# Drains of GpSimd behind every second row scatter of chunks 1 to 3, in place of register loads, in a fused Sinkhorn attention and mixture-of-experts kernel

## Chip, cores and metric

One core of a Trainium2 chip. The metric is the device time of one execution in microseconds (us), as the median of a kernel's runs. Two kernels are compared by the ratio of the mean time of one kernel's fast runs to that of the other's fast runs of the same rounds, so a ratio is not quite the ratio of the medians quoted beside it. "Faster", "same" and "slower" are set at 2%. Engine names in the profiles: PE is TensorE (PEld its weight loads), DVE VectorE, ACT ScalarE, POOL GpSimd, SP SyncE; POOLq is GpSimd's sequencer.

## What is computed

```python
# attention, B=4 H=8 S=768 D=64, 8 blocks of 96 rows
for _ in range(5):                       # Sinkhorn normalisation of sort_net -> P
    P = exp(P - max); P /= sum over rows; P /= sum over columns
k_sorted, v_sorted = P @ blocks of k, P @ blocks of v
attn_out = softmax(q_block @ k_sorted_block.T / sqrt(D)) @ v_sorted_block
x = attn_out as (3072, 512)
# mixture of experts, E=8, F=1024, one expert a row
e_idx = argmax(x @ w_gate + modality_bias[modality_id]); gate = softmax at e_idx
out[rows of e] = gate * (relu(x[rows of e] @ w1[e]) @ w2[e])
```

## The kernel before

The 3072 rows are made in four chunks of 768 (m = 0 to 3). Attention writes a chunk's rows into a row buffer `xb`, of which there are two; `place(m)` works out the row number in a scratch tensor for each row and scatters the chunk there with eight indirect DMAs from GpSimd. Rows of one expert then lie together. Slots (up to 256 rows of one expert) are read back with transposing DMAs on SP and go through the expert's two matrix products, which are laid between the later units of attention. Cuts are marked `# ...`.

```python
xb = [singles.tile([BLK, 8, GW], BF16, ...) for z in range(2)]      # two row buffers
small = ctx.enter_context(tc.tile_pool(name="small", bufs=1))       # one buffer unless said

def av(u):                                   # unit u of attention, 8 units a chunk
    xt = xb[(u // 8) % 2]
    # ... PE: op = attnT x v_sb
    nc.vector.reciprocal(rs, ...)                                    # L443
    nc.vector.tensor_tensor(xt[...], ov[...], rs..., ALU.mult)       # L444: writes the row buffer

def place(m):
    xt = xb[m % 2]
    dest = small.tile([BLK, 8], I32, tag="dest", ...)                # list of rows, one buffer
    # ... DVE works out dest; GpSimd puts the row's number into xt
    def one(t):
        if t:
            if m:
                for _ in range(2):
                    nc.gpsimd.reg_load(pause, etab[0:1, 0:1])        # L536
            nc.gpsimd.nop()
        ins = nc.gpsimd.indirect_dma_start(                          # L538
            out=xs_dram, out_offset=IndirectOffsetOnAxis(ap=dest[:, t:t + 1], axis=0),
            in_=xt.bitcast(I32)[:, t], in_offset=None)
        after = []                                                   # extra waits: none
        # ... the scatters are declared independent of each other
    for t in range(8):
        one(t)

def x_fetch(s, ...):                         # slot s, on SP, behind the chunk's scatters
    nc.sync.dma_start_transpose(out=xT_b[s % NX][...], in_=...)      # L661

def late_w1():                               # 2 MB of weights of the second expert, from GpSimd
    # ... load_w(1), behind the load of slot 1
at1(9, place, 0); at1(18, place, 1); at1(26, place, 2)               # at which unit of attention
at2(12, late_w1)                             # so the weights are issued just ahead of chunk 1's rows
```

The softmax here doesn't subtract the row's maximum and nothing guards it: scores larger than these inputs give would overflow.

Of the kernel before, what the change touches and what calls it, by code (L numbers as in the profile page):

```python
# [17 lines left out]
def kernel(  # L18
# [13 lines left out]
    nc = tc.nc  # L32
# [153 lines left out]
    etab = singles.tile([1, E], I32)  # L186
# [152 lines left out]
    def use(act=0.0, dve=0.0):  # L339
        busy[0] += act  # L340
        busy[1] += dve
# [150 lines left out]
        oh_t[m] = (oh, ls)  # L492

    scat = {}
    pause = nc.gpsimd.alloc_register("pause")
    ones_ = {}
    mark = [None]

    def place(m):
        oh, ls = oh_t[m]  # L500
        xt = xb[m % 2]
        prev = ohs[m % 2]
        rk = mipsum.tile([128, 8, E], FP32, tag="mi", name=f"rk{m}")
        rkf = rk.rearrange("p t e -> p (t e)")
        pb = bass.AP(tensor=prev.tensor, offset=prev.offset, ap=[prev.ap[0], [0, 8], prev.ap[1]])
        nc.tensor.matmul(rkf, maskUT[0:BLK, :], oh.rearrange("p t e -> p (t e)"), start=True, stop=False,
                         skip_group_check=True)
        nc.tensor.matmul(rkf, ones_bf[0:BLK, :], ebase.rearrange("p t e -> p (t e)"), start=False, stop=False,
                         skip_group_check=True)
        nc.tensor.matmul(rk, ones_bf[0:BLK, :], pb, start=False, stop=False, skip_group_check=True)  # L510
        for t in range(7):
            ob = bass.AP(tensor=oh.tensor, offset=oh[:, t].offset, ap=[oh.ap[0], [0, 7 - t], [1, E]])
            nc.tensor.matmul(rk[:, t + 1:8], ones_bf[0:BLK, :], ob, start=False, stop=(t == 6),
                             skip_group_check=True)
        sel_r = small.tile([BLK, 8, E], FP32, tag="selr", name=f"selr{m}")
        nc.vector.tensor_tensor(sel_r, rk[0:BLK], oh, ALU.mult)
        dest = small.tile([BLK, 8], I32, tag="dest", name=f"dest{m}")
        dstf = small.tile([BLK, 8], FP32, tag="dstf", name=f"dstf{m}")
        nc.vector.tensor_reduce(dstf, sel_r, AX.X, ALU.add)
        nc.vector.tensor_copy(dest, dstf)  # L520
        sm = small.tile([BLK, 8, 1], FP32, tag="sm", name=f"sm{m}")
        nc.vector.tensor_reduce(sm, ls, AX.X, ALU.add)
        gcol = xt.bitcast(FP32)[:, :, Dm // 2 + 1:Dm // 2 + 2]
        nc.vector.reciprocal(gcol, sm)
        g, hf = m // 2, m % 2
        icol = xt.bitcast(I32)[:, :, Dm // 2]
        idm = idI.rearrange("p (b f j) -> p b f j", b=4, f=2)[:, 2 * g:2 * g + 2, hf]
        nc.gpsimd.tensor_copy(icol.rearrange("p (r j) -> p r j", r=2), idm)
        scat[m] = []
        use(dve=1.5)  # L530

        def one(t):
            if t:
                if m:
                    for _ in range(2):
                        nc.gpsimd.reg_load(pause, etab[0:1, 0:1])  # L536
                nc.gpsimd.nop()
            ins = nc.gpsimd.indirect_dma_start(  # L538
                out=xs_dram, out_offset=bass.IndirectOffsetOnAxis(ap=dest[:, t:t + 1], axis=0),
                in_=xt.bitcast(I32)[:, t], in_offset=None)  # L540
            after = []
            tc.declare_no_dep(ins.ins, group="xs", reason="rows are disjoint", **({"keep": after} if after else {}))
            tc.add_to_no_dep_group("xs", ins.ins)
            for pre in after:
                tc.add_manual_dep(ins.ins, pre.name, SYNC, reason="rows leave at an even pace")
            scat[m].append(ins.ins)
        ones_[m] = one
        for t in range(8):
            one(t)
        nxt = ohs[(m + 1) % 2]  # L550
        ohsum = small.tile([BLK, E], FP32, tag="ohsum", name=f"ohsum{m}")
        nc.vector.tensor_reduce(ohsum, oh.rearrange("p t e -> p e t"), AX.X, ALU.add)
        nc.vector.tensor_tensor(nxt, ohsum, prev, ALU.add)
# [484 lines left out]
```

## Time and profile before

| | before |
|---|---|
| runs before the prediction | 193.73 us median (192.12 to 194.36, 3 runs) |
| profiled execution | 230.75 us, span 229.1 us, mean granted clock 0.856 |
| PE busy in the profile | 174.5 us |

The profiled execution is 37 us longer than the timed ones. Its run is not among them. In the timelines below a line is: start, duration, engine, source line, operation and tiles, count, and in brackets how long the engine had been idle and what ended that.

### The profile page before, as it was taken

To read this page: it belongs to the slowest core of one execution; us is meant where nothing else is said; L and a number is where in the kernel's file an instruction comes from. 1 tells how busy PE (TensorE), PEld (TensorE's weight loads), DVE (VectorE), ACT (ScalarE), POOL (GpSimd) and SP (SyncE) were. 2 spreads that over 40 slices of the span, in tenths; PEclk is the share of its full clock that TensorE was granted. 3 is DMA by queue.
4 is the path that set the end of the run, shared out by engine and by line. 5 is a ranking of instruction groups with operands and counts; after the bars stand their busy time and mean duration, and the time that the engine had idled before them with its cause. 6 is when DMAs were issued, how large, how long until landed. Compare 5 with 4: busy or idle time off the path is not lost.

```text
span 229.1 us, 5357 instructions
## 1 busy us (share of the span) xinstructions
PE 174.5 (76%) x2127; PEld 127.6 (56%) x2127; DVE 100.7 (44%) x332; ACT 93.4 (41%) x149; POOL 83.3 (36%) x118
## 2 busy tenths in 40 slices
PE   6573978876399986399954599933969999999930
PEld 6473877664299964167641477620456676675410
DVE  5877479643077885127740355430122322322200
ACT  2135678573178871356631544302223232232320
POOL 7801869406510317430177003572301322322330
PEclk9889799995557999569985599985799999999996
DMA  5999999999907399270032622452324346122210
GB/s 62 196 226 198 212 223 222 188 226 204 249 28 72 45 193 231 66 178 9 0 112 75 138 50 92 98 171 107 98 72 107 83 121 118 57 81 94 94 46 0
DMA packets 30164, 27.71 MB, mean 121 GB/s; under 512 B 18831, under 2 KB 25775, under 8 KB 29872
## 3 DMA queue, kind: packets, MB, share of 16 engines
q0 software_dynamic: 11792, 23.10, 45.2%
q1 hardware_dynamic: 18336, 4.16, 10.7%
q8 instruction: 19, 0.31, 0.5%
q14 instruction: 17, 0.14, 0.2%
HBM read 27.35 MB, written 10.52 MB: 165 GB/s over the span
## 4 chain that ended last, share of the span: by engine, by line
PE 33%; issue 27%; DMA 16%; DVE 9%; POOL 8%; another core or an unknown queue 1%; ACT 1%; POOLq 1%; DVEq 0%; ACTq 0%
DMA kvb<-in_v_dram 8%; DMA xs_scratch<-xb,dest 8%; POOL out_dram L708 6%; PE hp L694 6%; PE yp L717 5%; PE va L374 5%; DVE xb L444 4%; PE sc L417 4%; PE gt L453 4%; PE op L436 3%; PE lg L463 2%; PE tq L236 1%; PE ka L365 1%; POOL xs_scratch L538 1%
## 5 line engine op out<-in xcount | busy, mean ns | idle before, releaser
L708 POOL DMA_INDIRECT out_dram<-kvb,idg x25 | 24.5, 981 | 80.0 <-ACT kvb L704 38.2
L694 PE MATMUL hp<-xT,w 128*128 128x256 bf16 x384 | 49.1, 278 | 4.6 <-issue 2.5
L694 PEld LDWEIGHTS <-w 128*128 128x128 bf16 x384 | 36.7, 99 | 14.0 <-issue 6.1
L538 POOL DMA_INDIRECT xs_scratch<-xb,dest x32 | 29.4, 919 | 29.6 <-issue 27.4
L717 PE MATMUL yp<-w,hT 128*128 128x512 bf16 x96 | 26.9, 428 | 7.6 <-ACT hT L688 7.6
L423 ACT ACTIVATE attnT<-sc 96x768 bf16<-96x768 f32 x32 | 25.9, 810 | 15.0 <-PE sc L417 6.0
L717 PE MATMUL yp<-w,qT 128*128 128x512 bf16 x96 | 22.5, 379 | 0.0
L444 DVE TENSOR_TENSOR xb<-op,rs 96x512 bf16<-96x512 f32 x32 | 22.0, 687 | 1.2
L417 PE MATMUL sc<-qT,kT 64*128 64x96 bf16 (+1 forms) x256 | 13.8, 222 | 9.6 <-issue 6.1
L717 PEld LDWEIGHTS <-hT 128*128 128x128 bf16 x96 | 9.7, 106 | 20.0 <-ACT hT L688 9.3
L688 ACT ACTIVATE hT<-hp 128x512 bf16<-128x512 f32 x17 | 10.0, 595 | 26.4 <-remote 14.6
L706 DVE TENSOR_SCALAR kvb<-yp,idg 128x512 f32<-128x512 f32 x10 | 7.5, 751 | 29.5 <-PE yp L717 26.6
L704 ACT ACTIVATE kvb<-yp,idg 128x512 f32<-128x512 f32 x14 | 9.6, 687 | 22.8 <-PE yp L717 19.4
L688 ACT ACTIVATE qT<-hp 128x512 bf16<-128x512 f32 x16 | 9.5, 595 | 18.2 <-PE hp L694 18.1
L436 PE MATMUL op<-v_sb,attnT 96*128 96x65 bf16 x256 | 14.6, 204 | 2.6 <-DVE xb L444 2.0
L374 PE MATMUL va<-bd,kvb 128*128 128x128 bf16 x128 | 14.1, 283 | 2.3 <-DMA kvb<-in_v_dram 2.3
L352 ACT CAST kT<-ka 128x512 bf16<-128x512 f32 (+1 forms) x17 | 10.1, 639 | 14.0 <-PE ka L365 8.0
L417 PEld LDWEIGHTS <-kT 64*128 64x128 bf16 (+1 forms) x256 | 8.0, 102 | 13.6 <-issue 11.6
L717 PEld LDWEIGHTS <-qT 128*128 128x128 bf16 x96 | 9.2, 98 | 9.3
L374 PEld LDWEIGHTS <-kvb 128*128 128x128 bf16 x128 | 12.9, 189 | 2.6 <-DMA kvb<-in_v_dram 2.4
L453 PE MATMUL gt<-ident,xb 96*128 96x96 bf16 x128 | 9.6, 224 | 5.7 <-DVE xb L444 4.6
L436 PEld LDWEIGHTS <-attnT 96*128 96x128 bf16 x256 | 11.5, 105 | 3.3 <-DVE xb L444 2.5
(182 smaller groups left out, 233.3 us busy)
## 6 DMA issues: line engine op xcount, KB each, us to landing
w<-in_moe_w_dram POOLq DMA_DIRECT2D x4, 1024.0 KB
kvb<-in_k_dram POOLq DMA_DIRECT2D x4, 768.0 KB
kvb<-in_v_dram POOLq DMA_DIRECT2D x2, 1536.0 KB
q_in<-in_q_dram POOLq DMA_DIRECT2D x4, 384.0 KB
xs_scratch<-zpad SPq DMA_DIRECT2D x3, 258.0 KB
v_sb<-in_q_dram POOLq DMA_DIRECT2D x4, 192.0 KB
v_sb<-in_q_dram POOLq DMA_DIRECT2D x2, 384.0 KB
xs_scratch<-xb,dest POOLq DMA_INDIRECT x32
```

Of the source, the lines that this page charges most:

```text
L352: (nc.scalar.copy if pick(act, dve) else nc.vector.tensor_copy)(dst, src)
L374: nc.tensor.matmul(acc[:, z], v_cols[:, d0 + z], bd[g], start=True, stop=True)
L417: nc.tensor.matmul(sc[0:m, par, j * BLK:(j + 1) * BLK], kT[g][rows, x0:x0 + m], qT[rows, i], start=True, stop=True)
L423: mark[0] = nc.scalar.activation(attnT[u % 2][:, 0:8 * BLK].rearrange("p (r f) -> p r f", r=2), sc_tiles.pop(u)[0:BLK, :, 0:4 * BLK], ACT. ...
L436: nc.tensor.matmul(ov[:, par, j], attnT[u % 2][:, c0:c0 + 128], v_sb[g][0:BLK, par * 64 + h * 8 + i, 0:D + 1], start=True, stop=True)
L444: nc.vector.tensor_tensor(xt[:, :, h * D:(h + 1) * D].rearrange("p (r j) d -> p r j d", r=2), ov[0:BLK, :, :, 0:D], rs.broadcast_to([BLK, ...
L453: nc.tensor.transpose(tp[:, t], xb[m % 2][:, t, c * 128:(c + 1) * 128], ident[:BLK, :BLK])
L538: ins = nc.gpsimd.indirect_dma_start(out=xs_dram, out_offset=bass.IndirectOffsetOnAxis(ap=dest[:, t:t + 1], axis=0), in_=xt.bitcast(I32)[: ...
L688: mark[0] = nc.scalar.activation(dst, src, ACT.Relu)
L694: nc.tensor.matmul(hp[:, f], w_at(s, c * F + (2 * j + f) * 128, 128), xT_b[s % NX][:, c], start=(c == 0), stop=(c == 3))
L708: ins = nc.gpsimd.indirect_dma_start(out=out, out_offset=bass.IndirectOffsetOnAxis(ap=idg[:, t, 0:1], axis=0), in_=y, in_offset=None, boun ...
L717: nc.tensor.matmul(yp, hT_b[s % 2][:, fc, t * 128:(t + 1) * 128], w_at(s, 4 * F + fc * Dm, Dm), start=(fc == 0), stop=(fc == 7))
```

## The change

The register loads were meant to space a chunk's scatters. They are replaced by a `drain` of GpSimd before scatters 2, 4 and 6 of chunks 1, 2 and 3, nine in all, which should hold each further pair back until the engine is idle.

```diff
-    pause = nc.gpsimd.alloc_register("pause")
...
         def one(t):
             if t:
-                if m:
-                    for _ in range(2):
-                        nc.gpsimd.reg_load(pause, etab[0:1, 0:1])
+                if m and t % 2 == 0:
+                    nc.gpsimd.drain()
                 nc.gpsimd.nop()
```

Later lines move up by two: the drain is L534, the scatter L536, the slot load L659, the first expert product L692 (L694 before).

## The prediction

> **What bounds the kernel now.** I read the page first (shares by engine, slices), then the groups and the timeline of Pool for the scatters, then the uses and loads of the slots' tiles, then the timeline of PE and the busy times by window.
>
> Page, shares, slices and two groups:
>
> ```profile
> span 229.1 us, 5357 instructions
> PE 174.5 (76%) x2127; PEld 127.6 (56%) x2127; DVE 100.7 (44%) x332; ACT 93.4 (41%) x149; POOL 83.3 (36%) x118
> PE   6573978876399986399954599933969999999930
> POOL 7801869406510317430177003572301322322330
> ...
> L538 POOL DMA_INDIRECT xs_scratch<-xb,dest x32 | 29.4, 919 | 29.6 <-issue 27.4 <-DMA w<-in_moe_w_dram 2.0 <-POOL xb L528 0.3
> ```
>
> PE is the busiest engine. Its row of slices has four holes, and each lies under a run of sevens and fives of Pool: the row scatters of chunks 0 to 3. From slice 30 on PE is at nine tenths: the expert tail is bound by PE.
>
> Pool's timeline, four scatters of chunk 1 and the end of it:
>
> ```profile
> 84.86 0.98 POOL L538 DMA_INDIRECT xs_scratch<-xb,dest  x1 [5.58 <-issue]
> 86.14 0.95 POOL L538 DMA_INDIRECT xs_scratch<-xb,dest  x1 [0.30 <-issue]
> 87.39 0.91 POOL L538 DMA_INDIRECT xs_scratch<-xb,dest  x1 [0.30 <-issue]
> 88.61 0.91 POOL L538 DMA_INDIRECT xs_scratch<-xb,dest  x1 [0.30 <-issue]
> ...
> 93.46 0.90 POOL L538 DMA_INDIRECT xs_scratch<-xb,dest  x1 [0.30 <-issue]
> 97.18 1.01 POOL L708 DMA_INDIRECT out_dram<-kvb,idg  x1 [2.82 <-ACT kvb L704]
> ```
>
> A scatter takes 0.91 us on Pool and the next starts 0.30 us later, 1.21 us from start to start; eight take 93.46 + 0.90 - 84.86 = 9.50 us. Chunk 0, which has no register loads between its scatters, is no faster: in the same timeline its later ones start at 56.47, 57.70 and 58.92, 1.22 us apart. So the loads already cost nothing that Pool shows. The line of the loads says why:
>
> ```profile
> L536 POOLq EVENT_SEMAPHORE  x42: 17/17/17, 84.6 to 148.4; - x42
> L645 POOLq TENSOR_LOAD <-etab x3: 298/300/514, 34.8 to 62.8; - x3
> ```
>
> 42 = 3 chunks x 7 gaps x 2, so each register load is there only as a semaphore increment of 17 ns; a real load (of the weights' expert number, second line) is a TENSOR_LOAD of 300 ns. I read this as loads into a register that nobody reads, of which the compiler left only the count. The last increment is at 148.4 while the last scatter starts at 153.1: Pool's sequencer runs several scatters ahead of the engine, so whatever it does between them is hidden.
>
> **What the Trainium skill says.** (1) "Perfetto Trace Analysis", section "DMA Instruction — SWDGE (GPSIMD)": the sequencer is free once it has pushed such a DMA to the wait queue, and its recorded end is where the last descriptor is written, not where data lands. The trace agrees: the 4.7 us of run-ahead above, and records of 0.91 us against a median of 3.4 us to landing for the transfers of this scratch tensor. (2) "PSUM — Partial Sum Buffer", section "Engine vs sequencer instructions": a nop is the sequencer's alone and waits only for dispatch; "drain waits for the engine to go fully idle". No drain lies between the scatters of this trace, so its cost isn't shown here. (3) "DMA: Bandwidth & Descriptors", section "Latency and other measured facts": a floor of about 600 ns for a tensor_load. The trace has 300 ns for a real one and 17 ns for what is left of the pauses; the measurement decides, and removing them saves nothing.
>
> **The change, part by part.** Removed: 42 register loads, 42 x 17 ns = 0.7 us of a sequencer that is ahead anyway. On the path: 0.
>
> Added: drains before scatters 2, 4 and 6 of three chunks, nine in all. A drain stops the run-ahead: the next scatter is decoded only once the engine is idle. What a scatter costs from cold is in the trace at the head of each chunk: the vector engine writes the row numbers (timeline of DVE, line L520) from 83.50 for 0.17 us, and the first scatter of chunk 1 starts at 84.86, 1.19 us later; in chunk 3 143.28 + 0.17 to 144.62, 1.17 us. Part of that is the hand-over between engines, which a drain hasn't got. Against 0.30 us for a queued one a drain therefore costs at most 1.19 - 0.30 = 0.9 us; I choose two thirds, 0.6 us, as an estimate. Per chunk 3 x 0.6 = 1.8 us: eight scatters take 9.5 + 1.8 = 11.3 us. Over three chunks Pool is 5.4 us longer at work.
>
> Does it reach the end? Two things wait for a chunk's scatters: the loads of its slots on SP, and the output scatters behind them on Pool. Timeline of SP, the first load after chunks 1, 2 and 3, and below it the landing time from the view of this tile:
>
> ```profile
> 96.02 1.27 SPq L661 DMA_TRANSPOSE xT<-xs_scratch  x1
> 126.18 1.14 SPq L661 DMA_TRANSPOSE xT<-xs_scratch  x1
> 158.94 1.27 SPq L661 DMA_TRANSPOSE xT<-xs_scratch  x1
> DMA to landing us min/median/max: 3.2/4.3/5.5
> ```
>
> Landed about 100.3, 130.5 and 163.2. A slot takes 32 matmuls of line L694, so counting them in PE's timeline tells when a slot is first used: slot 2 (chunk 1), slot 4 (chunk 2), slot 8 (chunk 3):
>
> ```profile
> 115.92 1.05 PE L694 MATMUL hp<-xT,w 128*128 128x256 bf16 x8
> 146.80 3.65 PE L694 MATMUL hp<-xT,w 128*128 128x256 bf16 x32
> 183.63 1.91 PE L694 MATMUL hp<-xT,w 128*128 128x256 bf16 x16
> ```
>
> Slack: 15.6, 16.3 and 20.4 us. Against 1.8 us of delay (2.7 at most) nothing is late. The output scatters: one stands right behind chunk 2 (at 124.59) and two behind chunk 3 (154.34, 155.64), each with only 0.30 us of wait, so they slip by 1.8 us too; they read one of eight result buffers, and a buffer is written again four slots later, over 25 us on. Slack again. On the path: 0. The view of the chain that ended last does put 18.2 us on the transfer of chunk 3's rows, up to 170.38; I don't follow it there, since the Pool instruction at its end (174.44, L708) waits for a DVE result by Pool's own timeline. It is an inferred releaser.
>
> **The holes of PE.** Are they a cost in the timed runs, which the drains could change? In the profile PE advances in single matmuls 0.7 us apart during chunk 2, with "issue" as its wait, and ACT and DVE stand still too, until the scatters are over. By windows, the four holes:
>
> ```profile
> 50.00:64.00 14.00, 7.85 (x140) 6.13 (x141) 4.07 (x13) 5.08 (x9) 7.47 (x8) 0.52 1.12 213
> 84.00:97.00 13.00, 6.88 (x77) 4.22 (x76) 4.93 (x22) 3.79 (x7) 7.37 (x8) 0.79 0.76 155
> 115.00:129.00 14.00, 5.88 (x69) 3.69 (x69) 3.00 (x14) 3.83 (x6) 8.16 (x9) 0.64 0.40 112
> 150.00:160.00 10.00, 2.41 (x11) 0.62 (x9) 1.28 (x11) 1.68 (x3) 5.10 (x6) 0.65 0.45 146
> ```
>
> Columns: window, length, then busy time of PE, PEld, DVE, ACT, POOL, granted clock, DMA share, GB/s. PE idles 6.2 + 6.1 + 8.1 + 7.6 = 28.0 us there, and 229.1 - 174.5 - 28.0 = 26.6 us elsewhere. The timed runs have a median of 193.73 us, 35.4 us less than the profile. With PE's 174.5 us of work that leaves 19.2 us idle, less than the 26.6 us outside the holes. So in the timed runs the holes are largely or wholly gone: they come, I infer, with the taking of the profile. Then slack shrinks by the part of a hole that lies between scatter and use, at most 8 us, and stays above 7 us.
>
> **Rivals.** (a) The holes are in part real, and a burst of scatters starves the other engines. Then a break behind every second scatter lets them in. For: the code's own remark that rows should leave at an even pace, and holes exactly under the bursts, also where the DMA share is only 0.40. Against: the sum above. If 8 us of holes in chunks 1 to 3 were real and half went, the time would be 189.7 us. (b) The drain also waits for the rows to land, or restarts expensively. Then it costs about 3.4 us instead of 0.6, 3 x 3.4 = 10.2 us a chunk, which eats the reduced slack of chunk 1 (15.6 - 6 = 9.6 us) and perhaps of chunk 2, and the time would be 194.5 to 199 us. Against: a Pool instruction's record ends with its descriptors, and idle means the engine, not the transfers. (c) The stretched bursts leave the 2 MB load of the second expert's weights, which is in flight beside chunk 1, freer: its share of the DMA is mixed with the scatters between 84 and 94. It is used first at 102, so early arrival buys nothing: 193.7 us.
>
> **Range and chances.** Main path 0 us; I take 0.2 us off for rival (a) weighed against (b): 193.5 us. The three timed runs of before span 192.12 to 194.36, 1.2%, so noise alone takes a median about 1.5 us to either side; rival (a) stretches the range below to 190.3, rival (b) above to 196.5. Faster by over 2% (below 189.9) needs most of rival (a): 0.11. Slower by over 2% (above 197.6) needs rival (b) in full: 0.08. Within 2%: 0.81.
>
> **What would show it.** Right: the line of the loads is gone; scatters 2, 4 and 6 of chunks 1 to 3 start about 0.9 us after the end of the one before instead of 0.30, the others stay at 0.30; a chunk's eight take 11 to 12 us; slots 2, 4 and 8 still land over 5 us before their first matmul; PE has no new wait for the slots' tile; the tail from slot 5 on is as long as before. Wrong: gaps of 3 us or more at the drains (rival b), or timed runs below 190 us with PE's holes in chunks 1 to 3 shorter (rival a). A profile whose span moves while the timed runs don't would confirm that the holes belong to the profile.

## The result and the profile after

| | before | after |
|---|---|---|
| median of 4 runs | 193.22 us (192.12 to 194.36) | 199.74 us (198.78 to 202.02) |
| ratio | | 1.0321, 95% interval [1.0231, 1.041]: slower |
| profiled execution | span 229.1 us, clock 0.856 | span 200.3 us, clock 0.932 |

The page of the changed kernel, its span, busy times and the slices of PE and POOL:

```profile
span 200.3 us, 5324 instructions
...
PE 164.6 (82%) x2127; PEld 123.3 (62%) x2127; DVE 100.5 (50%) x332; ACT 93.2 (47%) x149; POOL 83.5 (42%) x118
...
PE   6484697977799798999129999797699999999980
...
POOL 7911479930572034004474335712374451313231
```

The profile got 29 us shorter while the timed runs got 6 us longer, so the two profiles are not of the same kind and mustn't be subtracted. Executions over 1.5% slower than the fastest of the same kernel are left out of the means. (The profiled run, 202.02 us, is the one of the four that counts as slow; e2, e13 and e14 below were profiled in fast runs and show like gaps in chunk 1.) Of the four holes of PE that the profile before showed, none is left, and a new one is there: the "12" in slices 20 and 21. First, the view of the line of the drains (count, then duration in ns: least, median, most):

```profile
L534 POOLq DRAIN  x9: 3410/4512/11810, 77.8 to 140.6; - x9
```

POOL's timeline of the changed kernel over chunk 1:

```profile
73.22 0.83 POOL L647 DMA_DIRECT2D w<-in_moe_w_dram  x1 [9.71 <-DMA xT<-xs_scratch]
74.05 0.94 POOL L649 DMA_DIRECT2D w<-in_moe_w_dram  x1
...
77.50 0.98 POOL L536 DMA_INDIRECT xs_scratch<-xb,dest  x1 [2.28 <-issue]
78.78 0.96 POOL L536 DMA_INDIRECT xs_scratch<-xb,dest  x1 [0.31 <-issue]
90.34 0.91 POOL L536 DMA_INDIRECT xs_scratch<-xb,dest  x1 [10.60 <-issue]
...
94.80 0.91 POOL L536 DMA_INDIRECT xs_scratch<-xb,dest  x1 [2.33 <-issue]
...
100.45 0.91 POOL L536 DMA_INDIRECT xs_scratch<-xb,dest  x1 [0.30 <-issue]
```

Each drain opens a gap of 2.32 to 10.60 us instead of 0.30. In chunk 1 the gaps are 10.60, 2.33 and 2.32 us, in chunk 2 3.60, 2.45 and 3.88, in chunk 3 4.12, 3.34 and 3.42. "Issue" as the releaser says only that the profile sees no semaphore there; the raw trace has more: sixteen semaphore updates for each transfer, of which the last marks its landing. The weights issued at 73.22 and 74.05 landed at 81.54 and 87.69, the first two scatters behind them at 88.11 and 88.31, and the first drain ended at 89.59. In all nine cases the drain ended after the last transfer that GpSimd had issued had landed, never before it: 0.12 us after in six, 0.32 in two, 1.28 in this one. The next scatter starts 0.75 us after the drain. The same holds for all 91 drains of the 14 profiled runs that have any (0.12 to 1.73 us, 59 of them 0.12). Transfers that SP issued don't hold it: in e3 a drain ended at 131.44 while a slot load, issued at 128.92, landed at 132.42.

Timeline of DVE, the two instructions on either side of its longest wait, and of PE, the one behind its hole:

```profile
94.76 0.20 DVE L443 RECIPROCAL rs<-op 96x8 f32<-96x8 f32 x1
103.21 0.69 DVE L444 TENSOR_TENSOR xb<-op,rs 96x512 bf16<-96x512 f32 x1 [8.25 <-issue]
```

```profile
103.96 0.62 PE L436 MATMUL op<-v_sb,attnT 96*128 96x65 bf16 x8 [8.01 <-DVE xb L444]
```

This is the first unit of chunk 3. It writes `xb[1]`, which chunk 1's scatters read, so in the compiled program DVE waits there for the landing of all eight of them; the last was written out at 101.36. PE needs what DVE frees and stands for 8 us. That is 1.2 times the whole loss of 6.5 us.

### The profile page after: what moved, and what is told of

Its sections match the earlier page's. It is cut to its first block, busy times and chain, and to the rows that moved or that the text cites.

```text
span 200.3 us, 5324 instructions
## 1 busy us (share of the span) xinstructions
PE 164.6 (82%) x2127; PEld 123.3 (62%) x2127; DVE 100.5 (50%) x332; ACT 93.2 (47%) x149; POOL 83.5 (42%) x118
## 4 chain that ended last, share of the span: by engine, by line
issue 44%; DMA 19%; POOL 17%; PE 7%; POOLq 6%; DVE 5%; DVEq 0%; SPq 0%
DMA kvb<-in_v_dram 9%; DMA xs_scratch<-xb,dest 8%; POOL out_dram L706 8%; POOL xs_scratch L536 7%; POOLq L534 5%; PE va L374 3%; DVE xb L444 2%; DMA xT<-xs_scratch 2%; PE hp L692 1%; DVE v_sb L352 1%; PE gt L453 1%; PE op L436 1%; POOL v_sb L120 1%; PE sc L417 1%; POOLq L1031 1%
## 5 line engine op out<-in xcount | busy, mean ns | idle before, releaser
L536 POOL DMA_INDIRECT xs_scratch<-xb,dest x32 | 29.5, 921 | 56.8 <-issue 53.9
L692 PE MATMUL hp<-xT,w 128*128 128x256 bf16 x384 | 48.4, 279 | 5.4 <-DMA xT<-xs_scratch 2.8
L692 PEld LDWEIGHTS <-w 128*128 128x128 bf16 x384 | 37.1, 100 | 14.2 <-issue 4.4
L423 ACT ACTIVATE attnT<-sc 96x768 bf16<-96x768 f32 x32 | 25.9, 810 | 15.6 <-PE sc L417 15.6
L715 PE MATMUL yp<-w,qT 128*128 128x512 bf16 x96 | 24.2, 399 | 0.0
L436 PE MATMUL op<-v_sb,attnT 96*128 96x65 bf16 x256 | 13.8, 198 | 10.7 <-DVE xb L444 10.1
L715 PE MATMUL yp<-w,hT 128*128 128x512 bf16 x96 | 22.5, 379 | 0.0
L436 PEld LDWEIGHTS <-attnT 96*128 96x128 bf16 x256 | 10.8, 101 | 11.6 <-DVE xb L444 10.8
L715 PEld LDWEIGHTS <-qT 128*128 128x128 bf16 x96 | 9.5, 101 | 10.3 <-issue 1.7
L374 PE MATMUL va<-bd,kvb 128*128 128x128 bf16 x128 | 13.5, 270 | 1.6 <-DMA kvb<-in_v_dram 1.6
L715 PEld LDWEIGHTS <-hT 128*128 128x128 bf16 x96 | 9.1, 98 | 9.1
L374 PEld LDWEIGHTS <-kvb 128*128 128x128 bf16 x128 | 12.6, 195 | 1.8 <-DMA kvb<-in_v_dram 1.7
L352 ACT CAST v_sb<-va 96x512 bf16<-96x512 f32 (+1 forms) x19 | 10.9, 614 | 4.1 <-PE va L374 3.1
L684 DVE TENSOR_SCALAR qT<-hp 128x512 bf16<-128x512 f32 x8 | 5.5, 691 | 14.2 <-PE hp L692 14.2
L242 ACT COPY qT<-tq 128x768 bf16<-128x768 bf16 x14 | 11.1, 794 | 3.0 <-PE tq L236 1.8
```

The lines of the kernel that those rows point to most:

```text
L242: eng(qT, tq.pop(u).rearrange("p t (i r) -> p i t r", r=16))
L352: (nc.scalar.copy if pick(act, dve) else nc.vector.tensor_copy)(dst, src)
L374: nc.tensor.matmul(acc[:, z], v_cols[:, d0 + z], bd[g], start=True, stop=True)
L423: mark[0] = nc.scalar.activation(attnT[u % 2][:, 0:8 * BLK].rearrange("p (r f) -> p r f", r=2), sc_tiles.pop(u)[0:BLK, :, 0:4 * BLK], ACT. ...
L436: nc.tensor.matmul(ov[:, par, j], attnT[u % 2][:, c0:c0 + 128], v_sb[g][0:BLK, par * 64 + h * 8 + i, 0:D + 1], start=True, stop=True)
L536: ins = nc.gpsimd.indirect_dma_start(out=xs_dram, out_offset=bass.IndirectOffsetOnAxis(ap=dest[:, t:t + 1], axis=0), in_=xt.bitcast(I32)[: ...
```

## The experiments

There were five chip jobs. In three (e0 to e3; e4 to e6 and e8; e13 to e16) the kernel before took about 194 us, in two (e7, e9 to e11; e17, e18) about 231 us, in all its runs. I call these the kind of 194 and the kind of 231; the timed runs of the result are of the first, the first profile of before is of the second. The kind went with the whole job, not with the kernel, couldn't be chosen, and one chip had both. Times are compared within a job only. Line numbers differ between runs, since some edits add or take lines.

| run | kind, median of before | this, us | ratio [95%] |
|---|---|---|---|
| e0 before, one look | 194.05 | 195.91 | |
| e1 neither loads nor drains | 194.05 | 194.44 | 1.0083 [1.0047, 1.0119] |
| e2 drains in chunk 1 | 194.05 | 201.05 | 1.0418 [1.0301, 1.0535] |
| e3 drains in chunks 2, 3 | 194.05 | 195.20 | 1.0053 [1.001, 1.0095] |
| e4 all drains, third row buffer | 194.24 | 202.31 | 1.0442 [1.0296, 1.0588] |
| e8 before, third row buffer | 194.24 | 194.07 | 1.0018 [0.9979, 1.0057] |
| e5 drain before scatter 2 of chunk 1 | 194.24 | 198.03 | 1.0257 [1.0159, 1.0356] |
| e6 drains before 4 and 6 of chunk 1 | 194.24 | 196.89 | 1.0217 [1.009, 1.0344] |
| e13 changed kernel again | 194.65 | 201.32 | 1.0454 [1.0362, 1.0546] |
| e14 all drains, row buffer and list freed | 194.65 | 201.93 | 1.0468 [1.0395, 1.0541] |
| e15 as e3 | 194.65 | 195.81 | 1.0078 [1.0035, 1.0121] |
| e16 drains in chunks 0, 2, 3 | 194.65 | 206.87 | 1.0731 [1.0632, 1.0831] |
| e10 as e14 | 231.27 | 210.57 | 0.911 [0.9063, 0.9158] |
| e11 all drains, list freed, one look | 231.27 | 210.94 | |
| e7 waits for landing, no drains | 231.27 | 212.56 | 0.9242 [0.9169, 0.9315] |
| e9 drain before scatter 6 of chunk 1 | 231.27 | 229.57 | 0.9872 [0.9826, 0.9918] |
| e17 all drains, weights behind chunk 1 | 230.81 | 226.80 | 0.9871 [0.9784, 0.9959] |
| e18 as e7 | 230.81 | 212.70 | 0.9233 [0.9149, 0.9318] |

### Whose is the loss: e0 to e3

e0 is the kernel before unaltered. Against the changed kernel, e1 leaves the drains out, e2 and e3 keep some:

```diff
-                if m and t % 2 == 0:        # e1: both lines out
+                if m == 1 and t % 2 == 0:   # e2
+                if m > 1 and t % 2 == 0:    # e3
                     nc.gpsimd.drain()
```

> The kernel before, unchanged, to get a second profile of it. Theory A (the profile of 229 us was an odd execution): span near 192 us, the four holes of PE are gone, and chunk 1's eight scatters run 0.30 us apart. Rival (taking a profile always makes those holes for this kernel): span near 229 us again with 28 us of holes, although the changed kernel's profile had none.

> The changed kernel with the drains taken out too: neither loads nor drains. Theory A (the removed loads cost nothing, the drains cost all): ratio to the kernel before 1.00, between 0.993 and 1.007. Rival (the small increments of the loads' semaphore did pace something): clearly above 1.01.

> Drains in chunk 1 alone (three of the nine). Theory A (the time goes through the row buffer: chunk 1's rows are still being read when the vector engine wants to write chunk 3's first unit into the same buffer, 8 us of idle PE): ratio 1.025 to 1.04, nearly the whole loss, with an idle of PE of about 8 us before the op matmuls in the profile. Rival B (the loss is in the slots' loads after chunks 2 and 3, or in Pool's sum of time, so about a third belongs to each chunk): ratio near 1.011.

> Drains in chunks 2 and 3 alone (six of the nine). Theory A: no buffer is written again after these chunks, only the first slot of chunk 2 can come late (1.45 us in the changed kernel's profile): ratio 1.000 to 1.010, no 8 us of idle before the op matmuls. Rival B (each chunk a third): ratio near 1.021.

e0's page, span and the slices of PE and POOL, then its POOL timeline over chunk 1:

```profile
span 194.2 us, 5346 instructions
...
PE   6494697988699979899999999959999999999900
...
POOL 7911387950273104575067635772123224232320
```

```profile
79.06 0.98 POOL L538 DMA_INDIRECT xs_scratch<-xb,dest  x1 [4.09 <-issue]
...
88.06 0.91 POOL L538 DMA_INDIRECT xs_scratch<-xb,dest  x1 [0.69 <-DMA xs_scratch<-xb,dest]
```

No hole: this is what the timed 194 us look like, with PE busy 163.3 us. Chunk 1 is out at 88.97 and is 9.0 us from its first start to its last. In this kernel the first unit of chunk 3 writes the row buffer at 96.59 without a wait.

e1 is 0.8% slower than before, just above what was expected (up to 1.007): taking the loads away is no gain, and if anything a small loss. e2 carries the whole loss, with PE waiting 8.0 us behind the row buffer; e3 has gaps of 2.3 to 4.5 us at its six drains and costs 0.5% (e15: 0.8%), no more than e1 without any drain. So the loss is chunk 1's alone, though the drains of chunks 2 and 3 are as real.

### Which drain: e5 and e6

```diff
+                if m == 1 and t == 2:        # e5
+                if m == 1 and t in (4, 6):   # e6
```

> One drain only, before scatter 2 of chunk 1. Theory L (a drain waits until everything that Pool has issued has landed, the weights of the second expert too): a gap of about 10.5 us, chunk 1's last scatter ends near 97.5 us, the vector engine waits 4 to 5 us for the row buffer, ratio 1.015 to 1.03. Rival F (a drain has a fixed cost of some 2.3 us and the 10.6 us were something else): gap near 2.3 us, ratio 1.00 to 1.008.

> Two drains, before scatters 4 and 6 of chunk 1. Theory L: the one before scatter 4 is now the first that meets the weights in flight and takes the long wait, a gap of about 7 to 8 us, the second 2.3 us; last scatter ends near 97 us, the vector engine waits 3 to 4 us, ratio 1.01 to 1.025. Rival F: both gaps 2.3 us, last scatter ends near 91.5 us, no wait, ratio 1.00 to 1.008.

Gaps: e5 10.50 us; e6 8.79 and 2.33 us. DVE's wait at the row buffer: 4.0 and 4.6 us, against 8.2 with all three. Whichever drain is the first of chunk 1 has the gap of 8.8 to 12 us (10.60 in the changed kernel, 12.00 in e4), so it isn't the place between the scatters that counts; the later ones add about 2.3 us each.

### Is the wait at the row buffer the cause: e4, e8, e14

e4 gives the changed kernel a third row buffer for chunk 3, in memory of a k tile that is no longer in use then; e8 gives it to the kernel before, as a control; e14 (and e10) has it and a second buffer for the list of rows:

```diff
+    xb.append(kT[0][0:BLK, 0:8 * GW].rearrange("p (t g) -> p t g", g=GW))
+    XB = (0, 1, 0, 2)                       # e4, e8, e10, e14
-        xt = xb[(u // 8) % 2]
+        xt = xb[XB[u // 8]]
-        dest = small.tile([BLK, 8], I32, tag="dest", ...)
+        dest = small.tile([BLK, 8], I32, tag="dest", ..., bufs=2)   # e10, e14 (e11: this alone)
```

> The changed kernel with all nine drains, but chunk 3's rows go to a third row buffer (over the key matrix of the first group, which is dead by then), so the vector engine need not wait for chunk 1's rows to be read. Theory A1 (the buffer is the only gate): no idle of 8 us before the op matmuls, ratio 1.00 to 1.01. Theory A2 (the buffer is the first of two gates; the rows of slot 2 land at 103.0 + 4.3 = 107.3 us in the changed kernel's profile, and PE would want them at 109.3 - 8.0 = 101.3): the 8 us turn into about 6 us of wait for slot 2's tile, ratio 1.02 to 1.03.

> The kernel before with the same third row buffer: the control for the run with the drains. Both theories: ratio 1.00 within 0.01; the wait is not there in the kernel before, so nothing is gained. If it were clearly faster, the buffer would have been a bound before as well.

> The changed kernel unaltered. If this job is of the kind in which the kernel before takes about 194 us (no holes in PE): ratio 1.025 to 1.045, DVE waits about 8 us ahead of its first write into the row buffer for the rows of chunk 3, and PE as long behind it. If it is of the kind in which the kernel before takes about 231 us: ratio 0.90 to 0.93, as with the doubled list. A rival for that kind (the doubled list did it, not the drains): above 0.95.

> All nine drains, third row buffer, doubled list of rows. Kind of 194 us: theory A4 (the two write-after-read waits were the whole loss) says ratio 1.00 to 1.012, no wait of DVE or PE of 3 us or more on row buffer, list or slot tile. Theory A3 (the late rows then hold up slot 2's tile) says 1.015 to 1.03 with PE waiting 3 to 6 us for the tile of slot 2. Kind of 231 us: 0.90 to 0.925 as in the run before of the same kernel.

e8 shows that the buffer itself is free (1.0018). But e4 is no faster than the changed kernel: neither of the two expected outcomes. Its longest wait, from the timeline of DVE:

```profile
105.40 0.17 DVE L521 CAST dest<-dstf 96x8 int32<-96x8 f32 x1 [8.38 <-DMA xs_scratch<-xb,dest]
```

The list of rows has one buffer, so chunk 2's list must wait for chunk 1's scatters too. With this freed as well (e14, in the same job as the changed kernel e13, which waits 7.98 us at the row buffer) no wait of DVE on either is left, and the time is still the same, 201.93 against 201.32 us. The timeline of PE in e14:

```profile
107.54 1.86 PE L694 MATMUL hp<-xT,w 128*128 128x256 bf16 x8 [7.31 <-DMA xT<-xs_scratch]
```

That is slot 2, the first slot with chunk 1's rows. Three waits for the same landing stand one behind the other within a few us, and taking away the first uncovers the next. The last one is no question of buffers: PE needs the rows. I had given 1.015 to 1.03 for that case (theory A3) and it measured 1.047, so its mechanism was right and its size too small. The row buffer, on which I had put the loss after the result, is where it shows and not why it is there.

The slot's own sum agrees. SP's load of slot 2 and PE's first use of it in e0, then the load in e14:

```profile
90.71 1.33 SPq L661 DMA_TRANSPOSE xT<-xs_scratch  x1
...
100.77 1.05 PE L694 MATMUL hp<-xT,w 128*128 128x256 bf16 x8
```

```profile
102.85 1.27 SPq L661 DMA_TRANSPOSE xT<-xs_scratch  x1
```

By the landing updates of the trace the load landed at 96.99 in e0, where PE first used it at 100.77: slack 3.8 us. In e14 it landed at 107.49, 10.5 us later, and PE started at 107.54. 10.5 - 3.8 = 6.7 us are left over; PE's first use moved by 107.54 - 100.77 = 6.8 us and the time by 201.93 - 194.65 = 7.3 us.

### Is it the weights ahead of the rows: e16, e17

```diff
+                if m != 1 and t % 2 == 0:    # e16: chunks 0, 2, 3
```

```diff
         for t in range(8):                  # e17: all drains, weights behind chunk 1's rows
             one(t)
+        if m == 1:
+            late_w1()
-    at2(12, late_w1)
```

> Drains in chunks 2 and 3 only. Kind of 194 us: ratio 0.998 to 1.012 as before (about 1.005). Kind of 231 us: two of four holes mended, so by the hole theory about half the gain, 0.94 to 0.97; if breaking any burst cured the whole execution it would be 0.90 to 0.925.

> Drains in chunks 0, 2 and 3, none in chunk 1. Kind of 194 us: if only the transfer of the weights ahead of chunk 1's rows makes a drain costly, 1.00 to 1.015; if a late chunk 0 costs too (slots 0 and 1 wait for it), 1.015 to 1.04 with PE waiting for the first slot's tile. Kind of 231 us: three of four holes mended, 0.90 to 0.94.

> All nine drains, but the weights of the second expert are issued behind chunk 1's eight scatters in place of ahead of them. Theory W (the drain waits for every transfer that Pool has issued, the weights too): chunk 1's three gaps are 2.3 to 5 us and none is near 10, its last scatter ends about 20 us after its first starts at most, and the first write of the row buffer for chunk 3 waits under 3 us on DVE. Rival P (the place in the program, not the weights, makes the first drain long): the first gap stays at 8 to 11 us. The time is no test of it, as the weights land 10 to 15 us later and slot 2 may wait for them: in the kind of 194 us 0.99 to 1.04.

Chunk 0 also has 2 MB of weights (the first expert's) ahead of it. In e16 its first drain opens 9.54 us, the others 2.66 and 2.32, and PE waits 11.5 us for the first slot's tile: 7.3% lost, more than chunk 1 costs. POOL and PE of e16:

```profile
64.30 0.92 POOL L536 DMA_INDIRECT xs_scratch<-xb,dest  x1 [9.54 <-issue]
...
80.62 1.65 PE L692 MATMUL hp<-xT,w 128*128 128x256 bf16 x7 [11.53 <-DMA xT<-xs_scratch]
```

In e17, the first drain of chunk 1 with no weights ahead, from POOL's timeline:

```profile
91.44 0.92 POOL L536 DMA_INDIRECT xs_scratch<-xb,dest  x1 [3.43 <-issue]
```

3.43, 2.35 and 2.34 us, as theory W said, and chunk 1 takes 16.7 us. So a drain's gap is 2.3 to 5.9 us behind scatters alone, as in chunks 2 and 3, and 8.8 to 12 us with 2 MB of weights in the queue. (One reserve: e17 fell in the kind of 231, where chunk 1 starts later; with the weights ahead the first gap there was 6.31 us in e11 and 7.58 in e10.) It's no remedy: slot 2 now waits for the weights.

```profile
111.38 1.89 PE L694 MATMUL hp<-xT,w 128*128 128x256 bf16 x8 [17.65 <-DMA w<-in_moe_w_dram]
```

### The kind of 231: e9, e10, e11, e7, e18

```diff
+                if m == 1 and t == 6:        # e9: one drain
```

```diff
-            after = []                       # e7, e18: no drains, a wait for the row before
+            after = [scat[m][t - 1]] if m and t and t % 2 == 0 else []
```

> One drain, before scatter 6 of chunk 1. Theory L: by then the weights have nearly landed; scatter 6 starts 5 to 6 us after the end of scatter 5, at about 91 us, the last scatter lands near 95 us, when the vector engine wants the row buffer: a wait of 0 to 1.5 us, ratio 1.00 to 1.01. If the ratio were above 1.015, a drain would cost beyond the gap that it makes.

> All nine drains, the third row buffer and a second buffer for the list of row numbers, whose single copy was the next thing the vector engine waited for (8.4 us) once the row buffer was free. Theory A3 (two write-after-read gates, and behind them the rows of slot 2): no long wait of the vector engine for chunk 1's scatters; PE waits instead for slot 2's tile, 4 to 7 us, ratio 1.015 to 1.03. Theory A4 (the two buffers were all): no long wait anywhere, ratio 1.00 to 1.01.

> All nine drains, a second buffer for the list of row numbers, but two row buffers as in the changed kernel. Theory A3: the row buffer comes first in the vector engine's order, so the 8 us of wait before the writing of the rows stay, time 199 to 202 us. If the list alone were the gate: time near 194 us.

> No loads and no drains; scatters 2, 4 and 6 of chunks 1 to 3 wait for the landing of the scatter just before them by its semaphore. Theory L (a drain waits for the landing of all that Pool has issued): gaps of the same pattern as with the drains, about 9 to 10.5 us for the first of chunk 1 (its rows queue behind the weights) and 1.5 to 3.5 us for the others, ratio 1.02 to 1.04. Rival F (a drain waits only for the engine and a fixed 2 us): then waiting for landings would differ clearly from the drains in the first gap of chunk 1.

> No drains; scatters 2, 4 and 6 of chunks 1 to 3 wait on the semaphore of the landing of the row before. If a drain is in effect such a wait: in the kind of 194 us ratio 1.03 to 1.05, first gap of chunk 1 9 to 11 us, the others 2 to 5 us, long wait of DVE ahead of the row buffer. If the drain costs more than the landing (a restart of Pool): 1.00 to 1.02 and gaps at least 1 us shorter. In the kind of 231 us: 0.92 to 0.93 as before.

These were written for the kind of 194 (but for e18's last sentence) and came back in the other, so the numbers expected don't apply; they answer another question. PE's timeline in e9, while chunk 2's eight scatters (113.71 to 123.14) run with no drain between them:

```profile
118.73 0.37 PE L692 MATMUL hp<-xT,w 128*128 128x256 bf16 x1 [0.45 <-issue]
119.45 0.38 PE L692 MATMUL hp<-xT,w 128*128 128x256 bf16 x1 [0.34 <-issue]
```

Single matmuls 0.7 us apart with no semaphore to wait for, then PE is idle for 5 us up to 127.68: the hole of the first profile again. The kernel before took 228 to 235 us in all its 23 runs of that job, so what goes with the holes is paid in timed runs as well; they don't come from taking a profile. The kinds already differ at chunk 0's scatters, which lie between 52 and 64 us in e0 and e9 alike. From 50 to 64 us GpSimd is busy 7.5 us in both and the DMA engines move 206 and 208 GB/s, but PE is busy 12.6 us in e0 and 7.4 in e9, DVE 10.3 and 4.6, ACT 11.1 and 4.4. So it isn't slower scatters or more traffic. The granted clock was lower too, 0.76 and 0.51; whether as cause or as consequence isn't shown. e10's page, the slices of PE and POOL:

```profile
PE   6576788785559998998928998599596999999990
...
POOL 7901669900741031224471447033372513131332
```

Chunk 0's hole, the "555", is left whole; there are no drains there. A shorter one, the "2" in slice 21 (105.2 to 110.5 us), lies at seven indirect DMAs in a row (102.40 to 111.06), three of results between two pairs of rows. Nine drains gain 9% in this kind (e10, and e11, which is the changed kernel but for the list), waits for landing 8% (e7 and e18), one drain in chunk 1 1% (e9, which lacks the register loads too, so that their going isn't the gain). In this kind it helps to break the runs of scatters, by drains or by waits; in the other kind there is nothing to break and all nine drains cost 3 to 5%.

A drain costs a wait for the landing, and a little more. In e7 and e18 a scatter starts 0.27 to 0.79 us after the landing that it waits for; behind a drain it is 0.12 to 1.73 us from landing to the drain's end, and 0.75 more. So the gaps of chunk 1 are 4.56, 2.25 and 1.73 us in e7, and 6.31, 2.33 and 2.32 in e11.

## Why the prediction was wrong

1. **The loads cost nothing: right.** Without them and without drains (e1) the time is not shorter but 0.8% longer.

2. **A drain costs 0.6 us, at most 0.9: wrong, and this is the step that failed.** It was sized by the restart of an idle GpSimd, on the reading that idle means the engine and not its transfers, which put rival (b) aside. The nine gaps measured 2.32 to 10.60 us, six of them over the 3 us that the prediction named as the sign of rival (b); a slowdown over 2% had been given a chance of 0.08. Chunk 1 was to be 1.8 us longer and is 10.60 + 2.33 + 2.32 - 3 x 0.30 = 14.35 us longer; all nine gaps, 36.1 us in sum less 9 x 0.30, make 33.4 us in place of 5.4. Rival (b), the wait for the landing, is what happens; its 3.4 us a drain fits chunks 2 and 3 (mean gap 3.5 us), but it too missed the weights in the queue ahead of chunk 1. With the measured 14.35 us in place of 1.8, the prediction's own least slack for slot 2 (15.6 - 8 = 7.6 us) would have given 14.35 - 7.6 = 6.7 us of loss, 200.4 us; 199.74 was measured. That it comes so close is partly luck: the slack was smaller (point 4), and so was the delay, as chunk 1 started 1.6 us earlier than in e0.

3. **"Two things wait for a chunk's scatters": incomplete.** There are four: slot loads, output scatters, the next but one chunk's writes into the row buffer, and the next chunk's list. In the changed kernel the row buffer's wait is the one that shows (8 us of PE). But e14 shows that with the two forgotten ones gone the loss is the same, so this gap in the list named the wrong place of the loss, not its size.

4. **Slack of 15.6 us, above 7 us in the timed runs: too large.** It came from a profile of the other kind. In e0 slot 2 has 3.8 us. That alone would have hidden the 1.8 us of delay that was predicted, so it isn't the step that failed, but it let through most of the real delay. Slot 4 of chunk 2 has 4.7 us in e0 (landed at 115.56, used at 120.28), and in e3 PE waits 3.2 us for it; yet e3 and e15 lose under 1%.

5. **"They come, I infer, with the taking of the profile": wrong as a reason, right for these runs.** e0's profile has no holes although it was taken in the same way. Its sum had PE busy for 174.5 us in the timed runs too; in e0 PE is busy 163.3 us and idle 30.9, more than the 26.6 that the prediction counted outside the holes, so the sum proved nothing. Holes belong to one kind of execution, which came for whole jobs, profiled and timed, at 231 us. There rival (a) fits, in that breaking the bursts helps: e10 gains 20.7 us, five times the 4 us that it was given. The runs that decided the prediction were of the other kind, where it is worth nothing.

**What stays open.** Why a job is of one kind or the other, and what stops the other engines in a long run of indirect DMAs, isn't known; no run was made for it. Waits for landing were not seen in the kind of 194, nor drains in chunks 2 and 3 alone in the kind of 231, nor the changed kernel itself there (e10 and e11 differ from it in buffers). Why most drains end 0.12 us after the last landing and others up to 1.73 is open too. No version beat the kernel before in the kind of 194; in the other e10 has the lowest ratio.

## What to carry to other kernels

Before pricing a drain on an engine that issues DMAs, count what that engine has in flight, large transfers ahead of it most of all, and then subtract the slack of everything that waits for what comes behind it: readers, writers of the buffers that are read, and the lists. When the profile's span and the timed runs differ by far more than the runs among themselves, treat the profile as another kind of execution, take slack from a profile whose span agrees, and try a change in both kinds before keeping or dropping it. When a freed buffer brings nothing, look for the next waiter on the same event before calling the cause found.

## What the Trainium skill lacked or had wrong

- "PSUM — Partial Sum Buffer", section "Engine vs sequencer instructions", has "drain waits for the engine to go fully idle". It doesn't say whether DMAs issued from the engine count. On GpSimd they do, by these runs: all nine drains of the changed kernel ended 0.12 to 1.28 us after the landing of the last transfer that GpSimd had issued, and lasted 3.4 to 11.8 us; a slot load that SP had issued was still under way at the end of a drain of e3.
- "DMA: Bandwidth & Descriptors", section "Latency and other measured facts": a tensor_load floor of about 600 ns; the records of the trace of before have 298, 300 and 514 ns. I found no page on what is left of register loads whose value nobody reads: here 42 of them left 42 semaphore records of 17 ns.
- "SBUF — State Buffer", section "SBUF: two separate sides", has contention between engines at the port pair that the vector engine and GpSimd share, and says that PE, ACT and the vector engine's own pair wait for no one. I found no page that has the kind of execution in which PE, ACT and DVE all nearly stop during a run of indirect DMAs (PE in single matmuls 0.7 us apart in e9; 231 against 194 us for the same kernel).
